# Blocks 2 and 3 of the first x tile: from TensorE transposes to a DMA transpose, with the first weight loads moved to ScalarE

## Chip, cores and metric

One Trainium2 chip; the kernel runs on one core. The metric is device time in microseconds (us), the median of several runs. Lower is better.

## The reference

```python
B, S, D, F = 1, 2048, 1024, 3584          # all bfloat16
def reference(x, w_gate, w_up, w_down):
    return (_gelu(x @ w_gate) * (x @ w_up)) @ w_down   # gelu, tanh form
```

## The kernel before

The 2048 tokens are worked in two halves of 1024, each in two blocks of 512 (`TB`). x is needed with its D axis on the partitions: `xT[tb]` holds eight blocks of 128 rows of D (block 0 is rows 0 to 127) by 512 tokens. For the gate and up products, F is cut into 28 tiles of 128 columns, loaded in chunks of four tiles (`load_w`; a chunk has a gate and an up part). The result stays on chip as `hT`, and the down projection follows for each half.

Most products run by a scheme of seven block products in place of eight (`quads`, `down_group`): sums of blocks of x (`t_sum`, on DVE and ACT) and of the weights (`s_sum`, on GpSimd) are made first. At the start these sums do not exist yet. `first_units` (from line 369) fills that time with plain products: for eight tiles of F and the first 512 tokens it runs over the eight blocks of D. These are the matmuls of line 355, 128x512 each, 16 for each set of two tiles and each of gate and up. I number them p1, p2, ... in the order of PE. The first four blocks' partial sum is also evacuated, since the later scheme uses it: `hold` (line 367), two ScalarE copies for each set and each of gate and up. The same bank then goes on to take blocks 4 to 7 (`rest`), which also ends in the gelu (line 313, ScalarE) and the multiplication (line 318, DVE).

What stands ahead of p1:

- Lines 228 to 236 issue the first loads, on SyncE and ScalarE alike: half of the tokens of x for blocks 0 and 1, weights for blocks 0 and 1 (256 columns; gate on SyncE, up on ScalarE), half of the tokens of x for blocks 2 and 3, the other 256 columns of the weights, and the weights for blocks 2 and 3. x lands untransposed in `xs0`.
- Line 254: seven matmuls on constants (`warm`, line 245) keep TensorE at work until x is there.
- `transpose_x0(0)` (line 337): eight 128x128 TensorE transposes into PSUM, copied to `xT` by DVE (line 345). `transpose_x0(1)` does the same for blocks 2 and 3 behind the first eight products, with one of its copies on ScalarE (line 347).
- Line 258: a DMA transpose (`load_xT`, line 214) brings blocks 4 to 7 on SyncE, and behind it in that queue come the chunk's remaining weights, chunk 1, the second token block of x (two more DMA transposes), and chunk 2.

The order on each engine is the order of the code: every instruction goes through a helper (`pe`, `act`, `dve`, `sp`, `pool`) that chains it behind the one before on its engine. A DMA also waits until the eighth one before it, in the order of the code, has landed, since eight semaphores are used in turn. Eight PSUM banks serve in pairs: `PB` 0 and 1, `VB` 2 and 3, `QB` 4 and 5, `RB` 6 and 7. Set 0 (tiles 0 and 1) uses VB and RB, set 1 (tiles 2 and 3) QB and PB; set 2 is again on QB and PB, set 3 on VB and RB.

In `first_units`, `top(n, j, k0, k1)` is set n, gate (j = 0) or up (j = 1), blocks k0 to k1 - 1, with `hold` where k1 is 4. KPQ is 2, KH is 4, KD is 8:

```python
transpose_x0(0); warm(RB[1], TB // 2)
top(0, 0, 0, KPQ); top(0, 1, 0, KPQ)          # p1-p8
transpose_x0(1)
top(1, 0, 0, KPQ)                             # p9-p12
top(0, 0, KPQ, KH); top(0, 1, KPQ, KH)        # p13-p20, two holds
top(1, 1, 0, KPQ)                             # p21-p24
top(1, 0, KPQ, KH); top(1, 1, KPQ, KH)        # p25-p32, two holds
outs(*rest(1)); outs(*rest(0))                # p33-p64
```

Of the kernel before, what the change touches and what calls it, by code (L numbers as in the profile page):

```python
# [34 lines left out]
def kernel(  # L35
# [8 lines left out]
    nc = tc.nc  # L44
# [6 lines left out]
    KH = KD // 2  # L51
# [5 lines left out]
    FG = 512  # L57
# [3 lines left out]
    TSB = TB // P  # L61
    XQ = 256
    NXQ = D // XQ
    KPQ = XQ // P
# [53 lines left out]
    PB, VB, QB, RB = (0, 1), (2, 3), (4, 5), (6, 7)  # L118
    last_on = {}

    def on(engine, inst):

        if engine in last_on:
            tc.add_manual_dep(
                inst.ins, last_on[engine].ins.name, SCHED_DEP, reason="engine order"
            )
        last_on[engine] = inst
        return inst

    def sp(inst):  # L130
        return on("sp", inst)

    def act(inst):
        return on("act", inst)

    def dve(inst):
        return on("dve", inst)
# [12 lines left out]
    def pe(inst):  # L150
        return on("pe", inst)
# [46 lines left out]
    def load_w(key, j, k0, k1, queue=sp, f0=0, f1=FG):  # L198

        c0 = key[1] * FG  # L200
        eng = nc.scalar if queue is act else nc.sync
        src = (wgv, wuv)[j][:, k0:k1, c0 + f0 : c0 + f1]
        queue(eng.dma_start(out=chunks[key][j][:, k0:k1, f0:f1], in_=src))

    def load_x0(q, queue, ts0=0, ts1=TSB):
        eng = nc.scalar if queue is act else nc.sync
        cols = slice(q * XQ, (q + 1) * XQ)
        src = x2[ts0 * P : ts1 * P, cols].rearrange("(ts p) d -> p ts d", p=P)
        queue(eng.dma_start(out=xs0[:, ts0:ts1, cols], in_=src))

    def load_xT(xT, h, tb, k0, k1):
        t0 = h * SH + tb * TB
        sp(
            nc.sync.dma_start_transpose(
                out=xT[tb][:, k0:k1, :],
                in_=xv[t0 : t0 + TB, k0:k1, :],
            )
        )
# [4 lines left out]
    xT = [None] * NTB  # L223
# [3 lines left out]

    FA = 2 * P
    first = (0, 0)
    for j, queue in enumerate((sp, act)):  # L230
        ts = slice(j * TSB // 2, (j + 1) * TSB // 2)
        load_x0(0, queue, ts.start, ts.stop)
        load_w(first, j, 0, KPQ, queue, 0, FA)
        load_x0(1, queue, ts.start, ts.stop)
        load_w(first, j, 0, KPQ, queue, FA, FG)
        load_w(first, j, KPQ, KH, queue)
    ident = const_pool.tile([P, P], BF16, name="ident")
    make_identity(nc, ident[:])

# [3 lines left out]
    def warm(bank, n=TB):  # L243
        pe(
            nc.tensor.matmul(  # L245
                banks[bank][:, 0:n],
                lhsT=warm_l,
                rhs=warm_r[:, 0:n],
                start=True,
                stop=True,  # L250
            )
        )
# [26 lines left out]
    def t_sum(name, c0=0, c1=KH, on_pool=False):  # L279
        def b(j, l):  # L280
            return xT[l][:, j * KH + c0 : j * KH + c1, :]

        t0 = ("t1", "t2", "t3", "b22", "t4").index(name) * KH * TB
        t = t_mem[:, t0 : t0 + KH * TB].rearrange("p (a b) -> p a b", b=TB)
        tsum[name] = t
        t = t[:, c0:c1, :]
        if name == "b22":
            for c in range(c1 - c0):
                act(nc.scalar.copy(out=t[:, c, :], in_=b(1, 1)[:, c, :]))
            return  # L290
        in0, in1 = {
            "t1": lambda: (b(0, 1), b(0, 0)),
            "t2": lambda: (b(1, 1), tsum["t1"].bitcast(F32)[:, c0:c1, :]),
            "t3": lambda: (b(1, 1), b(0, 1)),
            "t4": lambda: (b(1, 0), tsum["t2"].bitcast(F32)[:, c0:c1, :]),
        }[name]()
        if on_pool:
            pool(nc.gpsimd.tensor_tensor(out=t, in0=in0, in1=in1, op=ALU.subtract))
            return
        dve(nc.vector.tensor_tensor(out=t, in0=in0, in1=in1, op=ALU.subtract))  # L300
# [4 lines left out]
    def gelu(ps, last=False):  # L305

        if last:
            g_sb = new_o(F32)
        else:
            e0 = 4 * CH + (g_ctr[0] % 4) * 2 * TB  # L310
            g_ctr[0] += 1
            g_sb = w_mem[:, e0 : e0 + 2 * TB].bitcast(F32)
        act(nc.scalar.activation(out=g_sb, in_=ps[:], func=ACT.Gelu_apprx_tanh))  # L313
        return g_sb

    def mult(hT, g_sb, ps, fc, tb):
        dve(
            nc.vector.tensor_tensor(  # L318
                out=hT[:, fc, tb * TB : (tb + 1) * TB],
                in0=g_sb,  # L320
                in1=ps[:],
                op=ALU.mult,
            )
        )

    def transpose_x0(q):

        parts = [(KPQ * q, 0, 4), (KPQ * q + 1, 0, 4)]
        over = (QB[1], PB[1])
        if q == 0:  # L330
            parts = [(0, 0, 2), (0, 2, 4), (1, 0, 4)]
            over = (PB[0], PB[1], QB[0])
        for n, (kd, ts0, ts1) in enumerate(parts):
            tp = banks[over[n]][:].bitcast(BF16)
            for ts in range(ts0, ts1):
                pe(
                    nc.tensor.transpose(  # L337
                        tp[:, ts * P : (ts + 1) * P],
                        xs0[:, ts, kd * P : (kd + 1) * P],
                        ident[:],  # L340
                    )
                )
            cols = slice(ts0 * P, ts1 * P)
            if q == 0 or n == 0:
                dve(nc.vector.tensor_copy(out=xT[0][:, kd, cols], in_=tp[:, cols]))
            else:
                act(nc.scalar.copy(out=xT[0][:, kd, cols], in_=tp[:, cols]))

    def plain_products(held, tiles, j, k0, k1):
        for kd in range(k0, k1):  # L350
            for u, t in enumerate(tiles):
                w_sb = chunks[(0, t // FPG)][j]
                f0 = t % FPG * P
                pe(
                    nc.tensor.matmul(  # L355
                        banks[held[u][j]][:],
                        lhsT=w_sb[:, kd, f0 : f0 + P],
                        rhs=xT[0][:, kd, :],
                        start=kd == 0,
                        stop=kd in (KH - 1, KD - 1),  # L360
                        skip_group_check=True,
                    )
                )

    def hold(held, tiles, j):
        for u, t in enumerate(tiles):
            act(nc.scalar.copy(out=p_hold(t, j), in_=bank2(held[u][j])))

    def first_units(hT):

        gs = {}

        def gelus(held, tiles):
            for u, t in enumerate(tiles):
                gs[t] = gelu(banks[held[u][0]])

        def outs(held, tiles):
            for u, t in enumerate(tiles):
                mult(hT, gs[t], banks[held[u][1]], t, 0)

        sets = ((VB, RB), (QB, PB), (QB, PB), (VB, RB))

        def top(n, j, k0, k1):
            tiles = (2 * n, 2 * n + 1)
            plain_products(sets[n], tiles, j, k0, k1)
            if k1 == KH:
                hold(sets[n], tiles, j)

        def rest(n):
            tiles = (2 * n, 2 * n + 1)  # L390
            plain_products(sets[n], tiles, 0, KH, KD)
            gelus(sets[n], tiles)
            plain_products(sets[n], tiles, 1, KH, KD)
            return sets[n], tiles

        transpose_x0(0)
        warm(RB[1], TB // 2)
        top(0, 0, 0, KPQ)
        top(0, 1, 0, KPQ)
        transpose_x0(1)  # L400
        top(1, 0, 0, KPQ)
        top(0, 0, KPQ, KH)
        top(0, 1, KPQ, KH)
        top(1, 1, 0, KPQ)
        top(1, 0, KPQ, KH)
        top(1, 1, KPQ, KH)
        outs(*rest(1))
        outs(*rest(0))
        for j in range(2):
            top(2, j, 0, KH)  # L410
        for j in range(2):
            top(3, j, 0, KH)
        t_sum("t1", 0, KH // 2)
        t_sum("t1", KH // 2, KH)
        t_sum("t2")
        outs(*rest(2))
        t_sum("t3", 0, KH // 2)
        t_sum("b22")
        outs(*rest(3))
        t_sum("t3", KH // 2, KH)  # L420
        t_sum("t4", 0, KH // 2)
        t_sum("t4", KH // 2, KH)
        for j in range(2):
            s_sum(0, MID[0], j, "s3")
        for j in range(2):
            for name in ("s1", "s2"):
                s_sum(0, MID[0], j, name)
        for j in range(2):
            s_sum(0, MID[0], j, "s4")
# [772 lines left out]
```

## Time and profile before

| what | value |
|---|---|
| median of 3 runs | 537.33 us (537.15 to 537.83) |
| profiled execution: time | 538.38 us |
| profiled execution: span, first to last instruction | 536.6 us |
| PE (TensorE matmul) busy | 531.6 us, 99% of the span |
| DVE, ACT, POOL busy | 375.8, 274.2, 257.9 us |
| DMA traffic over the span | 102.69 MB, 191 GB/s |
| p1 starts, p33 starts, p65 starts | 4.78, 13.14, 20.07 us |

Times in a view count from the span's start. PE is TensorE's matmuls, PEld its weight loads, DVE the vector engine, ACT the scalar engine, POOL GpSimd, SP SyncE, and a q behind an engine's name its DMA issues or its other queue work. The chain that ended last is followed back from the last instruction to whatever released each step. A DMA's time to landing counts from the start of its issue.

### The profile page before, as it was taken

How to read it: one execution, taken by the hardware profiler on the slowest of the kernel's cores; microseconds unless marked ns; L12 is line 12 of the kernel's file. 1: busy time of each engine (PE TensorE's matmuls, PEld its weight loads, DVE VectorE, ACT ScalarE, POOL GpSimd, SP SyncE). 2: the span in 40 equal slices, each digit the busy share in tenths (PEclk: the TensorE clock that was granted, in tenths of full speed). 3: DMA queues.
4: the chain of work that ended last, by engine and by line, in shares of the span. 5: the costliest groups of instructions: out<-in, count | busy, mean ns of one | idle time of the engine just before them, and what ended most of it. 6: DMA issues, size and time to landing. Idle time of an engine off the chain costs nothing.

```text
span 536.6 us, 6968 instructions
## 1 busy us (share of the span) xinstructions
PE 531.6 (99%) x2360; PEld 382.4 (71%) x2380; DVE 375.8 (70%) x457; ACT 274.2 (51%) x471; POOL 257.9 (48%) x202
## 2 busy tenths in 40 slices
PE   9999999999999999999999999999999999999997
PEld 4448888887767686776768677776768686766866
DVE  1389988989799997988655343344445469969961
ACT  3466666666464229118455554655555551452280
POOL 0078999998499300000056494958668670000000
PEclk9999999999999999999999999999999999999999
DMA  8973845489892987789941322405041339677946
GB/s 214 267 263 114 240 141 153 120 234 284 227 369 94 346 289 271 241 277 293 327 161 35 123 83 76 133 25 156 1 156 37 121 97 334 215 249 243 290 144 213
DMA packets 97746, 102.69 MB, mean 191 GB/s; under 512 B 18224, under 2 KB 72624, under 8 KB 97712
## 3 DMA queue, kind: packets, MB, share of 16 engines
q1 hardware_dynamic: 73328, 83.57, 49.1%
q10 hardware_dynamic: 24384, 18.68, 11.6%
q8 instruction: 19, 0.31, 0.2%
q14 instruction: 15, 0.12, 0.1%
HBM read 85.98 MB, written 12.58 MB: 184 GB/s over the span
## 4 chain that ended last, share of the span: by engine, by line
PE 98%; DMA 1%; issue 0%; ACT 0%
PE bank L511 60%; PE bank L793 31%; PE bank L355 5%; DMA t_mem<-t_dram 1%; PE bank L245 1%; PE bank L337 0%; ACT o_sb L849 0%
## 5 line engine op out<-in xcount | busy, mean ns | idle before, releaser
L511 PE MATMUL bank<-t_mem,s_mem 128*128 128x512 f32 x1096 | 252.0, 391 | 0.0
L511 PEld LDWEIGHTS bank<-t_mem,s_mem 128*128 128x128 f32 x1096 | 205.7, 188 | 43.6
L462 POOL TENSOR_TENSOR s_mem<-w_mem 128x512 fp32r<-128x512 bf16 x80 | 100.6, 1276 | 177.0 <-DVE t_mem L300 94.7
L318 DVE TENSOR_TENSOR hT<-w_mem,bank 128x512 bf16<-128x512 f32 x106 | 71.0, 683 | 69.7 <-PE bank L511 39.9
L527 DVE TENSOR_TENSOR bank<-bank,m 128x512 f32<-128x512 f32 x112 | 72.3, 693 | 43.3 <-ACT m L567 40.6
L793 PE MATMUL bank<-t_mem,s_mem 128*128 128x512 f32 x416 | 98.4, 394 | 0.2 <-DMA t_mem<-t_dram 0.2
L313 ACT ACTIVATE w_mem<-bank 128x512 f32<-128x512 f32 x106 | 62.6, 597 | 56.8 <-DVE bank L527 36.0
L793 PEld LDWEIGHTS bank<-t_mem,s_mem 128*128 128x128 f32 x416 | 78.0, 188 | 17.7 <-issue 0.6
L511 PE MATMUL bank<-xT,w_mem 128*128 128x512 bf16 x311 | 70.3, 379 | 0.5
L691 DVE TENSOR_TENSOR t_mem<-w_mem 128x1024 fp32r<-128x1024 bf16 x56 | 66.6, 1236 | 0.9 <-PE bank L511 0.9
L462 POOL TENSOR_TENSOR s_mem<-w_mem,s_mem 128x512 fp32r<-128x512 bf16 x46 | 65.5, 1445 | 3.2 <-PE bank L511 3.2
L511 PEld LDWEIGHTS <-w_mem 128*128 128x128 bf16 x320 | 30.6, 98 | 38.0 <-issue 2.4
L462 POOL TENSOR_TENSOR s_mem<-s_mem,w_mem 128x512 fp32r<-128x512 f32 x46 | 55.6, 1229 | 0.2
L572 ACT COPY bank<-bank 128x512 f32<-128x512 f32 x56 | 32.0, 571 | 26.5 <-PE bank L511 21.2
L475 ACT CAST s_mem<-w_mem 128x512 fp32r<-128x512 bf16 x48 | 29.5, 617 | 24.7 <-PE bank L511 23.5
L567 ACT COPY m<-bank 128x512 f32<-128x512 f32 x56 | 32.8, 588 | 15.9 <-PE bank L511 15.9
L793 PEld LDWEIGHTS <-hT 128*128 128x128 bf16 x224 | 21.2, 98 | 26.7 <-issue 2.1
L858 ACT CAST o_sb<-bank 128x512 bf16<-128x512 f32 x27 | 14.8, 586 | 33.8 <-PE bank L793 33.8
L793 PE MATMUL bank<-t_mem,s_late 128*128 128x512 f32 (+1 forms) x132 | 30.3, 382 | 0.0
L537 ACT COPY bank<-bank 128x512 f32<-128x512 f32 x40 | 22.8, 571 | 12.0 <-PE bank L511 12.0
L765 DVE TENSOR_TENSOR s_mem<-hT 128x512 fp32r<-128x512 bf16 (+2 forms) x28 | 23.0, 840 | 8.1 <-PE bank L793 8.1
L793 PEld LDWEIGHTS bank<-t_mem,s_late 128*128 128x128 f32 x132 | 24.4, 188 | 4.9
(61 smaller groups left out, 399.4 us busy)
## 6 DMA issues: line engine op xcount, KB each, us to landing
t_mem<-t_dram SPq DMA_DIRECT2D x56, 512.0 KB, 5.5
wd_sb<-in_w_down_dram SPq DMA_DIRECT2D x26, 512.0 KB, 7.2
t_dram<-o_sb SPq DMA_DIRECT2D x14, 512.0 KB, 3.4
w_mem<-in_w_gate_dram ACTq DMA_DIRECT2D x6, 1024.0 KB, 5.5
w_mem<-in_w_up_dram ACTq DMA_DIRECT2D x6, 1024.0 KB, 7.9
w_mem<-in_w_gate_dram SPq DMA_DIRECT2D x9, 512.0 KB, 5.8
w_mem<-in_w_up_dram SPq DMA_DIRECT2D x9, 512.0 KB, 7.7
w_mem<-in_w_down_dram SPq DMA_DIRECT2D x4, 1024.0 KB, 6.8
```

The lines of the kernel that those rows point to most:

```text
L313: act(nc.scalar.activation(out=g_sb, in_=ps[:], func=ACT.Gelu_apprx_tanh))
L318: nc.vector.tensor_tensor(out=hT[:, fc, tb * TB : (tb + 1) * TB], in0=g_sb, in1=ps[:], op=ALU.mult,)
L355: nc.tensor.matmul(banks[held[u][j]][:], lhsT=w_sb[:, kd, f0 : f0 + P], rhs=xT[0][:, kd, :], start=kd == 0, stop=kd in (KH - 1, KD - 1), s ...
L462: pool(nc.gpsimd.tensor_tensor(out=t, in0=in0, in1=in1, op=op))
L475: act(nc.scalar.copy(out=t, in_=a(1, 1)))
L511: nc.tensor.matmul(banks[bank][:], lhsT=lhs[:, c, :], rhs=rhs[:, c, :], start=start and c == 0, stop=c == KH - 1, skip_group_check=True,)
L527: nc.vector.tensor_tensor(out=banks[dst][:], in0=banks[src][:], in1=m5[:], op=ALU.add)
L567: act(nc.scalar.copy(out=m5[j][:], in_=banks[V_[j]][:]))
L572: act(nc.scalar.copy(out=banks[R_[j]][:], in_=banks[Q_[j]][:]))
L691: dve(nc.vector.tensor_tensor(out=t, in0=in0, in1=in1, op=ALU.subtract))
L765: dve(nc.vector.tensor_tensor(out=t, in0=in0, in1=in1, op=op))
L793: nc.tensor.matmul(banks[bank][:, c0:c1], lhsT=lhs(i, u), rhs=rhs(i)[:, c0:c1], start=start and i == 0, stop=stop and i == NS - 1, skip_gr ...
```

## The change

SyncE now issues, in this order: half of the tokens of x for blocks 0 and 1; a DMA transpose of blocks 2 and 3, all 512 tokens (256 KB), straight into `xT`; the gate weights and the up weights for blocks 2 and 3; and then, as before, the DMA transpose of blocks 4 to 7 and all that follows. ScalarE issues the other half of x and then the four quarter parts of the weights for blocks 0 and 1. x for blocks 2 and 3 is no longer loaded untransposed, and the second set of eight TensorE transposes and their two copies are gone. The sixteen products on blocks 0 and 1 (both sets, gate and up) now come first, the sixteen on blocks 2 and 3 behind them, so that the four holds follow each other. All from `rest(1)` on has its order.

```diff
-    for j, queue in enumerate((sp, act)):
-        ts = slice(j * TSB // 2, (j + 1) * TSB // 2)
-        load_x0(0, queue, ts.start, ts.stop)
-        load_w(first, j, 0, KPQ, queue, 0, FA)
-        load_x0(1, queue, ts.start, ts.stop)
-        load_w(first, j, 0, KPQ, queue, FA, FG)
-        load_w(first, j, KPQ, KH, queue)
+    load_x0(0, sp, 0, TSB // 2)
+    load_xT(xT, 0, 0, KPQ, KH)
+    load_x0(0, act, TSB // 2, TSB)
+    for f0 in (0, FA):
+        for j in range(2):
+            load_w(first, j, 0, KPQ, act, f0, f0 + FA)
+    for j in range(2):
+        load_w(first, j, KPQ, KH)
...
-    def transpose_x0(q):
-
-        parts = [(KPQ * q, 0, 4), (KPQ * q + 1, 0, 4)]
-        over = (QB[1], PB[1])
-        if q == 0:
-            parts = [(0, 0, 2), (0, 2, 4), (1, 0, 4)]
-            over = (PB[0], PB[1], QB[0])
-        for n, (kd, ts0, ts1) in enumerate(parts):
+    def transpose_x0():
+
+        over = (PB[0], PB[1], QB[0])
+        for n, (kd, ts0, ts1) in enumerate(((0, 0, 2), (0, 2, 4), (1, 0, 4))):
...
-            if q == 0 or n == 0:
-                dve(nc.vector.tensor_copy(out=xT[0][:, kd, cols], in_=tp[:, cols]))
-            else:
-                act(nc.scalar.copy(out=xT[0][:, kd, cols], in_=tp[:, cols]))
+            dve(nc.vector.tensor_copy(out=xT[0][:, kd, cols], in_=tp[:, cols]))
...
-        transpose_x0(0)
+        transpose_x0()
         warm(RB[1], TB // 2)
-        top(0, 0, 0, KPQ)
-        top(0, 1, 0, KPQ)
-        transpose_x0(1)
-        top(1, 0, 0, KPQ)
-        top(0, 0, KPQ, KH)
-        top(0, 1, KPQ, KH)
-        top(1, 1, 0, KPQ)
-        top(1, 0, KPQ, KH)
-        top(1, 1, KPQ, KH)
+        for k0 in (0, KPQ):
+            for n in range(2):
+                for j in range(2):
+                    top(n, j, k0, k0 + KPQ)
```

## The prediction

> **What bounds the kernel now.** I read the page first. PE is busy for 531.6 of 536.6 us, and the chain that ended last is PE for 98%; so only PE's own instructions and the moments at which PE waits count.
>
> ```profile
> PE 531.6 (99%) x2360; PEld 382.4 (71%) x2380; DVE 375.8 (70%) x457; ACT 274.2 (51%) x471; POOL 257.9 (48%) x202
> ...
> PE 98%; DMA 1%; issue 0%; ACT 0%
> ```
>
> The change touches the first 20 us alone. So next came the timeline of PE, and that of the weight loads (PEld), which show waits that matmuls hide:
>
> ```profile
> 0.77 3.15 PE L245 MATMUL bank<-const-bfloat16-1.0 128*128 128x512 bf16 x7 [0.77 <-PEq L1186]
> 3.71 1.06 PE L337 MATMUL bank<-ident,w_mem 128*128 128x128 bf16 x8
> 4.57 0.42 PE L245 MATMUL bank<-const-bfloat16-1.0 128*128 128x256 bf16 x1
> 4.78 2.79 PE L355 MATMUL bank<-xT,hT 128*128 128x512 bf16 x8
> 7.41 0.61 PE L337 MATMUL bank<-ident,w_mem 128*128 128x128 bf16 x8
> ...
> 6.49 0.58 PEld L355 LDWEIGHTS <-hT 128*128 128x128 bf16 x3 [0.28 <-issue]
> 7.19 0.65 PEld L337 LDWEIGHTS <-w_mem 128*128 128x128 bf16 x8
> 7.80 0.59 PEld L355 LDWEIGHTS <-hT 128*128 128x128 bf16 x4
> 8.81 0.76 PEld L355 LDWEIGHTS <-hT 128*128 128x128 bf16 x5 [0.43 <-DMA hT<-in_w_gate_dram]
> ```
>
> Columns: start, length, engine, line, instruction; in brackets the idle time before and what ended it. PE is never idle after 0.77. Products p1 to p5 start at 4.78, 5.21, 5.63, 6.06 and 6.49, that is 0.43 us apart; from p6 on the step is 0.216 (64 products from 20.07 to 33.89). PE thus runs at half speed until about 6.6 us. One wait is visible: p13's weights land late (8.81), which makes its step 0.31 instead of 0.216. Third, the queues:
>
> ```profile
> 0.74 0.45 SPq L209 DMA_DIRECT2D w_mem<-in_x_dram  x1
> 1.24 0.46 SPq L203 DMA_DIRECT2D hT<-in_w_gate_dram  x1
> ...
> 4.69 4.21 SPq L214 DMA_TRANSPOSE xT<-in_x_dram  x1
> 8.96 0.57 SPq L203 DMA_DIRECT2D hT<-in_w_gate_dram  x1
> ```
>
> The four-block transpose holds SyncE for 4.21 us, 1.05 a block, and the gate weights for rows 512 to 1023 leave only behind it.
>
> **The change, part by part.** Times are those of the profiled execution: span 536.6, 538.38 in all.
>
> *Removed from PE:* the second set of eight transposes. It takes PE from 7.41 to 7.85: **-0.44**. With it go one copy on DVE (0.42) and one on ACT (0.59); neither is on the chain.
>
> *p13's wait* (0.31 - 0.216 = 0.10) goes: those weights, issued at 3.62 and landed 5.1 us later, are now first read by p17, at 7.19 + 9 x 0.216 = 9.13: **-0.10**.
>
> *The order* puts four evacuations of ACT (L367, two copies each) behind p20, p24, p28 and p32, which are 4 x 0.216 = 0.86 us apart. A pair of copies takes more:
>
> ```profile
> 9.67 1.07 ACT L367 COPY hT<-bank 128x512 f32<-128x512 f32 x2 [1.03 <-PE bank L355]
> 10.63 0.61 ACT L367 COPY s_late<-bank 128x512 f32<-128x512 f32 x1
> ```
>
> Two copies start 9.67, the third 10.63: 0.48 each, 0.96 a pair. Before, four other products lay between the second and third pair, and ACT caught up. After: the first copy starts 0.04 after p19's end (9.56 + 0.38), at 9.98; the sixth at 9.98 + 5 x 0.48 = 12.38, and ends 0.61 later, 12.99. p34 overwrites that bank, and would be ready at 7.19 + 26 x 0.216 = 12.81; it starts near 13.04. Before, the sixth copy (the second of the pair 12.26 + 1.07) ended at 13.33 and p34 started at 13.39, 0.03 behind its turn. **+0.2**. All PE work behind queues on it.
>
> *Weights from ScalarE.* p1 needs its gate weights by 4.57 (its weight load). Before, they were SyncE's second issue (1.24, landed after 3.2, at 4.42); now they are ACT's second, whose row is 1.25 and 3.4, so 4.67, and p1 comes 0.1 late. Bounds: nothing, and what an ACT issue loses beside transposes. ACT's 512 KB gate loads show that: issued at 72.00, 90.08 and 108.22,
>
> ```profile
> hT<-in_w_gate_dram ACTq DMA_DIRECT2D x1, 512.0 KB, 4.1
> ...
> hT<-in_w_gate_dram ACTq DMA_DIRECT2D x1, 512.0 KB, 5.9
> ...
> w_mem<-in_w_gate_dram ACTq DMA_DIRECT2D x1, 512.0 KB, 5.4
> ```
>
> The first has no transpose near; the others were issued while SyncE issued two (at 89.19 and 90.38; at 107.82 and 109.81): 1.3 to 1.8 more. But there a 512 KB load of w_down was also ahead. A lone block, issued at 134.79, sends its first packets at 136.0, 1.2 us on; so the gate issue, at the same moment as the transpose, should be ahead of most of it. I take **+0.2**, between 0 and +1.8. The next weights are needed later each time: up by 6.4, second gate part 7.4, up 8.2. ACT's third and fourth issues landed at 1.79 + 4.8 = 6.6 and 2.31 + 5.1 = 7.4 behind x, which now isn't ahead of them; the fifth was never so early. I take no wait; at worst 0.2.
>
> *The transpose, blocks 2 and 3.* Issue 1.24 + 2 x 1.05 = 3.35; the four-block one landed 2.1 us after its issue ended (4.69 + 6.3 = 11.0 against 8.90), so about 5.5; p17 needs it at 9.13. Rows of any transpose run from 2.7 us (one block, 134.79) to 9.3 (14.86, behind 2 MB of weights): 3.9 to 10.5. I take no wait; at most +1.4. It is one queue, so no transpose waits for another.
>
> *SyncE behind it.* It loses two x and two weight issues and gains 2.1 us: two 256 KB weight issues end near 4.4 (the second needs ACT's x, landed 3.9), the four-block transpose starts near 4.45 instead of 4.69 and ends at 8.66. The gate weights behind it landed at 12.54; now 12.3, and p33 needs them at 7.19 + 25 x 0.216 = 12.59. If the short transpose takes 0.6 longer to issue, p33 waits 0.3; between nothing and +0.5. Chunk 1 was issued at 11.22, landed 6.8 later, and is read at 20.07: 2 us to spare.
>
> Sum: -0.44 - 0.10 + 0.2 + 0.2 = **-0.15 us**. Later PE work moves with it: the one later wait of PE is 0.2 us for a DMA whose issue follows PE. The profiled execution (538.38) is 1.05 above the median (537.33). Forecast: 538.2 for such an execution, **537.2** as a median, 536.7 to 537.9 by this case alone. About 0.2% (1.07 us) is what a measurement of this kernel can tell from no change.
>
> **Rivals.**
>
> *Full gain.* Nothing is late and the copies overlap more: -0.54, 536.8. For it: x's second load, whose two halves took 4.7 and 4.8 us against 2.9 and 3.2 for the first, leaves the queues. Against: the copies' 0.96. It stays within 0.2%.
>
> *The first weights queue behind the transpose (slower).* Place: p1. Price: the 1.3 to 1.8 above put the landing at 6.0 to 6.5, p1 late by 1.4 to 1.9; with the -0.34 of the other terms that is +1.1 to +1.6, 538.4 to 538.9. It makes the kernel measurably slower from a lateness of 1.4 us. PE is then also idle while still at half speed. If full speed waits for unbroken work (0.77 to 6.6, 5.8 us, here), starting over costs up to 5.8/2 = 2.9 more. For it: both rows. Against: the w_down load ahead of both.
>
> The Trainium skill (DMA: Bandwidth & Descriptors, Issuing engines are not separate DMA queues) says that issues of ScalarE and SyncE run on the same 16 DMA engines and interleave, and that two issuers save only issue time; this speaks against what the move to ScalarE could give, and the two rows agree. The Trainium skill (TensorE: Matmul & The Clock Gate, Part 1) says that full speed comes after a busy window of about 3.4 us that runs freely; by it, one missed window would cost an estimated 3.4/2 = 1.7 us, and where the window falls changes from run to run.
>
> *The transpose lands late.* Place: p17. At the 9.3 row, +1.4 - 0.34: 538.4. Against: 3.6 us of slack over the 5.5.
>
> **How the numbers follow.** Forecast 0.62; full gain 0.10; weights behind the transpose 0.20; late transpose 0.04; other, either side, 0.04. Slower by over 0.2%: nine tenths of the second rival, half of the third, some of the rest: 0.22. Faster by over 0.2% needs 1.07 of a possible 0.54, so only an earlier full speed gives it: 0.06. Within: 0.72. Range 536.4 (full gain and some scatter) to 538.9 (the second rival without the speed's loss).
>
> **What would show it.** PE's timeline: eight transposes, then p1 at 4.8 to 5.0 (5.9 or later: second rival); the 0.43 us steps end near 6.6; sixteen products without a break; no idle ahead of p17 (else third rival); a step of about 0.4 at p34; DMA rows: ACT's second issue landing after some 3.4 us, SyncE's short transpose holding it for 2.1. Wrong if the first 20 us gain or lose over 0.5 us elsewhere, or if anything past 34 us changes.

## The result and the profile after

The changed kernel takes 538.62 us (median of 11 runs, 538.02 to 539.93) against 537.48 for the kernel before (11 runs, 537.15 to 538.60): ratio 1.0020, 95% interval 1.0011 to 1.0028. It is slower, by 1.1 us. A repeat (e13 below) gave 538.48 against 537.61, ratio 1.0021 (1.0012 to 1.0030).

The page of the changed kernel's profile (span 536.9, time 538.65) shows PE less busy (531.6 before), and 1% of the chain that ended last is now on ACT:

```profile
PE 530.5 (99%) x2352; PEld 382.0 (71%) x2372; DVE 376.7 (70%) x456; ACT 273.4 (51%) x470; POOL 258.9 (48%) x202
...
PE 97%; DMA 1%; ACT 1%; issue 0%; ACTq 0%
```

In its lines L334, L349, L361 and L500 are what L337, L355, L367 and L511 were. The timeline of PE (start, length, instruction, idle time before):

```profile
3.71 1.06 PE L334 MATMUL bank<-ident,w_mem 128*128 128x128 bf16 x8
4.57 0.42 PE L246 MATMUL bank<-const-bfloat16-1.0 128*128 128x256 bf16 x1
4.78 1.17 PE L349 MATMUL bank<-xT,hT 128*128 128x512 bf16 x4
7.10 13.45 PE L349 MATMUL bank<-xT,hT 128*128 128x512 bf16 x59 [1.15 <-DMA hT<-in_w_up_dram]
```

and that of the weight loads:

```profile
5.14 0.31 PEld L349 LDWEIGHTS <-hT 128*128 128x128 bf16 x2 [0.21 <-issue]
7.09 1.41 PEld L349 LDWEIGHTS <-hT 128*128 128x128 bf16 x8 [1.64 <-DMA hT<-in_w_up_dram]
```

p1 is not late. p1 to p4 take 1.17 us, since full speed (0.216 us a product) starts with p2 (5.14) in this execution. p5 would follow at 5.78; it starts at 7.10, because the first up weights land at 7.05. The chain in order of time (start, length, what; idle pieces are "issue") says which issue that is, and shows the copies:

```profile
1.79 5.26 DMA hT<-in_w_up_dram
7.05 0.05 issue
7.10 3.50 PE bank L349 x15
10.59 0.02 issue
10.62 1.07 ACT hT L361 x2
11.69 0.03 ACT s_late L361
11.72 0.34 issue
12.05 1.60 ACT hT L361 x3
13.66 0.04 issue
13.70 0.38 PE bank L349
```

It is ScalarE's third issue (1.79). Behind p19 ACT's copies carry the chain as far as p34, which starts at 13.70, 0.26 behind its turn (p33 at 13.22, and 0.216 for it). SyncE's queue:

```profile
0.74 0.45 SPq L209 DMA_DIRECT2D w_mem<-in_x_dram  x1
1.25 1.33 SPq L214 DMA_TRANSPOSE xT<-in_x_dram  x1
...
4.00 5.11 SPq L214 DMA_TRANSPOSE xT<-in_x_dram  x1
9.15 0.58 SPq L203 DMA_DIRECT2D hT<-in_w_gate_dram  x1
```

The two profiles differ by only 0.3 us (538.65 - 538.38; p65 at 20.39 and 20.07), the medians by 1.1. The experiments had to explain the rest too. In nearly all profiles below, time less p65's start is 518.2 within 0.4 (519.3 in e13), so p65's start is a fair reading of a profiled execution. It is a reading of that execution alone, not of the median.

### The profile page after: what moved, and what is told of

It is laid out like the page before. It is cut to its first block, busy times and chain, and to the rows that moved or that the text cites. A ratio compares the mean times of both kernels' runs of the same rounds, so it can differ in the third digit from the quotient of the medians.

```text
span 536.9 us, 6944 instructions
## 1 busy us (share of the span) xinstructions
PE 530.5 (99%) x2352; PEld 382.0 (71%) x2372; DVE 376.7 (70%) x456; ACT 273.4 (51%) x470; POOL 258.9 (48%) x202
## 4 chain that ended last, share of the span: by engine, by line
PE 97%; DMA 1%; ACT 1%; issue 0%; ACTq 0%
PE bank L500 60%; PE bank L782 33%; PE bank L349 4%; DMA hT<-in_w_up_dram 1%; ACT hT L361 0%; ACTq L203 0%; ACTq L209 0%; ACT o_sb L838 0%; ACT s_late L361 0%
## 5 line engine op out<-in xcount | busy, mean ns | idle before, releaser
L500 PE MATMUL bank<-t_mem,s_mem 128*128 128x512 f32 x1096 | 252.0, 391 | 0.0
L500 PEld LDWEIGHTS bank<-t_mem,s_mem 128*128 128x128 f32 x1096 | 205.8, 188 | 43.5
L451 POOL TENSOR_TENSOR s_mem<-w_mem 128x512 fp32r<-128x512 bf16 x80 | 101.7, 1293 | 176.2 <-DVE t_mem L301 94.6
L500 PE MATMUL bank<-xT,w_mem 128*128 128x512 bf16 x310 | 70.3, 379 | 0.5
L500 PEld LDWEIGHTS <-w_mem 128*128 128x128 bf16 x320 | 30.6, 98 | 38.0 <-issue 2.4
```

The costliest lines, as they stand in the source:

```text
L451: pool(nc.gpsimd.tensor_tensor(out=t, in0=in0, in1=in1, op=op))
L500: nc.tensor.matmul(banks[bank][:], lhsT=lhs[:, c, :], rhs=rhs[:, c, :], start=start and c == 0, stop=c == KH - 1, skip_group_check=True,)
```

## The experiments

Each timed run is a median of 11 or 12 executions beside before's on the same chip; intervals are about 0.09% (0.5 us) either side, so only what profiles and times say together is used.

**What moves from run to run.** e1 and e9 are the kernel before, unchanged; e10 and e13 the changed kernel.

> The kernel before, once more, for a second profile. In its first profile the half-speed steps of TensorE (0.43 us) lasted until 6.6 us; in that of the changed kernel full speed began at 5.1 us, so that the two profiles differ by 0.3 us where the medians differ by 1.1. If the start of full speed moves from run to run (theory: chance of the run), a second profile shows it elsewhere between some 4 and 7.5 us, and the span moves by up to 0.8 us with it; the time stays within 0.3 us of before. If the change itself brought full speed forward (rival), it is at 6.6 us again.

537.81 against 537.66, ratio 1.0001 (0.9992 to 1.0010). Its profile (538.19) has full speed from 6.5 again: the rival's reading for now.

> A third profile of the kernel before. Theory: two things vary from run to run in the first 9 us, when full speed starts (6.6 and 6.5 us in the first two profiles) and when the gate weights of blocks 2 and 3 land (8.8 and 7.6 us), and p13 starts at the later of the two; a run near the median (537.5) has p13 near 8.0, against 8.8 and 8.4 in the two profiles, which were of slow runs (538.4, 538.2). Then time less p65's start is 518.2 within 0.4 in this one too. Rival: the first 20 us are the same in all runs and the spread comes from later.

537.91. Timeline of PE:

```profile
4.72 1.93 PE L355 MATMUL bank<-xT,hT 128*128 128x512 bf16 x8
7.09 0.68 PE L337 MATMUL bank<-ident,w_mem 128*128 128x128 bf16 x8 [0.43 <-DMA w_mem<-in_x_dram]
7.83 6.46 PE L355 MATMUL bank<-xT,hT 128*128 128x512 bf16 x28
```

Here full speed starts by 5.2, but the early start is lost again: the second transposes wait for x's second load (landed 7.22). p13 came near 8.7, not 8.0 as expected. p65 is at 19.96. So the start of full speed does move (6.6, 6.5, 5.2, and 4.7 in e4), and the kernel before has a wait for a third issue of its own.

> A second profile of the changed kernel. Theory: ScalarE's up weights land at 6.8 to 7.3 us again and p5 starts there, whether full speed starts early or not; p65 at 20.2 to 20.5. Rival: the late landing was a chance of one run, and p5 starts before 6.6.

538.00. Here ScalarE's third issue took 4.3 us, and p5 started at 6.15, 0.4 late: p65 at 19.68. The rival holds; the landing varies by chip or by execution.

> The changed kernel once more, on the chip of the three runs beside it. Theory (p5 starts at the landing of ScalarE's third issue, and this moves from run to run: 7.05 and 6.10 us in its two profiles): slower than before by 0.4 to 1.3 us, and p5's wait in the profile agrees with the time within 0.4. Rival (the loss is a chance of the first call): within 0.2 of before.

538.48, ratio 1.0021 (1.0012 to 1.0030). The up weights landed at 6.86, p5 started at 6.91, 1.1 late, and p34 again 0.26 late. The profiled execution (539.46) also lost 0.3 us at 55.7 and 0.5 at 269.1, which the two other profiles of the changed kernel do not show.

**What makes p5 wait.** The edits are against the changed kernel, except in e5. The first puts the up weights that p5 reads on SyncE, ahead of the transpose.

```diff
     load_x0(0, sp, 0, TSB // 2)
+    load_w(first, 1, 0, KPQ, sp, 0, FA)
     load_xT(xT, 0, 0, KPQ, KH)
...
-    for f0 in (0, FA):
-        for j in range(2):
-            load_w(first, j, 0, KPQ, act, f0, f0 + FA)
+    load_w(first, 0, 0, KPQ, act, 0, FA)
+    for j in range(2):
+        load_w(first, j, 0, KPQ, act, FA, FG)
```

> The changed kernel, but the up weights of the first 256 columns (128 KB) are SyncE's second issue, ahead of the short transpose, and no longer ScalarE's third. Theory (the wait of p5 for these weights is the whole loss, 1.3 us): they land near 4.7 us, p5 follows p4 without a break, and the time is 1.0 to 1.4 us under the changed kernel's, that is from 0.4 under to 0.1 above before. Rival (anything late only moves the wait on): p9 waits for the next gate weights, now ScalarE's third issue, which land at 7.0 or later, and less than 0.6 us is won back.

537.94 against 537.66, ratio 0.9998 (0.9989 to 1.0007): the loss is gone. But the waits moved on, as the rival said, though to p13 and p33 and not to p9; the timeline of PE:

```profile
4.78 3.28 PE L350 MATMUL bank<-xT,hT 128*128 128x512 bf16 x12
8.38 4.49 PE L350 MATMUL bank<-xT,hT 128*128 128x512 bf16 x20 [0.32 <-DMA hT<-in_w_up_dram]
13.12 1.25 PE L350 MATMUL bank<-xT,hT 128*128 128x512 bf16 x4 [0.25 <-DMA hT<-in_w_gate_dram]
```

p5 follows p4; p13 waits 0.48 and p33 0.41. With the copies repaired too (below, e14's edit):

> Both repairs: the up weights that p5 reads as SyncE's second issue ahead of the transpose, and the second copies on DVE. Theory: no wait of p5 and none of p34; what remains are p13's and p33's waits for weights behind the transposes (0.5 and 0.4 us in the profile of the first repair alone); time 0.2 to 0.6 us under before. Rival (each wait only moves on): within 0.15 of before or above it.

538.62 against 537.61, ratio 1.0016 (1.0007 to 1.0025). My theory fell: p13 waited 1.06 us for ScalarE's fourth issue (landed 8.41, 6.1 us after it) and p33 0.17. Those weights landed no earlier in e2 (8.34), so the profiles do not explain why e2's median is 0.7 lower; the two ran on different chips. Putting one weight load ahead of the transpose is no reliable repair.

Next, the transpose behind the plain weight loads:

```diff
     load_x0(0, sp, 0, TSB // 2)
-    load_xT(xT, 0, 0, KPQ, KH)
...
     for j in range(2):
         load_w(first, j, KPQ, KH)
+    load_xT(xT, 0, 0, KPQ, KH)
```

> The changed kernel, but the short transpose is issued behind the two 256 KB weight loads for blocks 2 and 3 on SyncE, so that ScalarE's issues run beside plain loads alone. Theory A (the transpose's packets hold the DMA engines, and ScalarE's third issue lands 5.3 us after its issue for that reason): the up weights land at 6.0 us or before, p5 waits 0.3 us at most, p17 waits for the transpose (landing 7.5 to 9), and the time is 0.7 to 1.3 us under the changed kernel's. Theory B (a third issue on a queue takes some 5 us whatever is beside it, as x's second load took 4.8 before): they land at 6.6 us or later again and p5 waits 0.9 us or more.

538.26 against 537.66, ratio 1.0013 (1.0004 to 1.0021). Theory B holds: with 512 KB of weights in the transpose's place the up weights still landed at 6.69, and p5 started at 6.74, 1.03 late.

A plain load of the same x in its place (the comment stands for the edit of the products, which is left out):

```diff
-    load_xT(xT, 0, 0, KPQ, KH)
+    load_x0(1, sp, 0, TSB)      # x plain, 256 KB; second PE transposes behind p8, p9 to p16 as in the change
```

> The changed kernel's queues and order of products, but in the short transpose's place SyncE issues a plain 256 KB load of the same x, and TensorE transposes it behind p8 as before. Theory (third issue): ScalarE's up weights land at 6.5 to 7.1 again and p5 waits 0.8 to 1.4 us with full speed early. Rival (the transpose's packets): they land by 6.0. Either way what is left against the changed kernel's 5.3 us to landing is the transpose's part. Time: within 0.4 us of the changed kernel's by the theory, 1 us or more under it by the rival.

538.27 against 537.47, ratio 1.0017 (1.0008 to 1.0026). The up weights landed at 6.54; p1 waited too (5.39; its gate weights landed at 5.34), which hid p5's wait. e7, on the same chip, has the transpose in that place and landed them at 7.10: 0.56 later. DMA in the stretch 3.2 to 5.6 us, first of the changed kernel, then of e6 (q10 is ScalarE's queue: packets, MB, share of the engines):

```profile
DMA packets 1319, 0.41 MB, mean 169 GB/s; under 512 B 1018, under 2 KB 1319, under 8 KB 1319
...
q10 hardware_dynamic: 320, 0.15, 36.6%
```

```profile
DMA packets 1254, 0.74 MB, mean 308 GB/s; under 512 B 65, under 2 KB 1254, under 8 KB 1254
...
q10 hardware_dynamic: 679, 0.33, 49.4%
```

About the same number of packets, but the transpose's are of 256 bytes. All queues together moved 0.33 MB less in 2.4 us, and ScalarE's queue less than half as much. The 0.56 is not the price of a transpose at equal bytes, though: the plain load takes SyncE less time to issue, so that e6 has another 256 KB of weights (issued at 1.75, in e7 at 2.63) ahead of the up weights (1.79).

The kernel before with a swap on ScalarE's queue alone, x's second half load and the first up weights:

```diff
-        load_w(first, j, 0, KPQ, queue, 0, FA)
+        if j == 0:
+            load_w(first, j, 0, KPQ, queue, 0, FA)
         load_x0(1, queue, ts.start, ts.stop)
+        if j == 1:
+            load_w(first, j, 0, KPQ, queue, 0, FA)
```

> The kernel before with one swap on ScalarE's queue: x's second load is its second issue, and the up weights that p5 reads its third (as in the changed kernel). No transpose, no other change. Theory (a queue's third issue at the start lands 4 to 5 us after it, at 5.8 to 6.7, whatever is beside it): p5 waits for them, by 0.1 to 1.0 us depending on when full speed starts, its step is above 0.5 us in the profile, and the time is 0.2 to 0.8 us above before. Rival (only the transpose makes the third issue late): they land by 5.5, p5's step stays at 0.43 or 0.22 and the time is that of before.

537.69 against 537.47, ratio 1.0002 (0.9994 to 1.0011). The up weights landed at 6.20 and p5 waited 0.45, as the theory said; the time did not follow, because p13 waits for the gate weights of blocks 2 and 3 (8.82) in this order anyway.

The last one holds SyncE's transpose, and all behind it on SyncE, until the fifth warm matmul has ended:

```diff
     load_x0(0, sp, 0, TSB // 2)
-    load_xT(xT, 0, 0, KPQ, KH)
...
-    for j in range(2):
-        load_w(first, j, KPQ, KH)
...
     for i in range(NWARM):
         warm(i)
+        if i == 4:
+            held_back = last_on["pe"]
+    load_xT(xT, 0, 0, KPQ, KH)
+    tc.add_manual_dep(last_on["sp"].ins, held_back.ins.name, SYNC_DEP, reason="held back")
+    for j in range(2):
+        load_w(first, j, KPQ, KH)
```

> The changed kernel, but SyncE's short transpose, and all behind it on SyncE, wait for the fifth of the seven warm matmuls (end at 3.1 us), so that ScalarE's issues have only x ahead of and beside them until then. Theory (what counts is how many bytes are ahead: 768 KB when the up weights land 6.5 to 7.1, 512 KB here): ScalarE's third issue lands by 5.7 and p5 waits 0.1 us at most; in exchange the four-block transpose is issued 1.2 us later and p33 waits for the weights behind it, 0.5 to 1.3 us, so that the time is within 0.5 of the changed kernel's. Rival (the rank in the queue counts): it lands at 6.2 or later and p5 waits 0.5 us or more.

537.81 against 537.98, ratio 1.0000 (0.9991 to 1.0008): no loss. This run tells the rank in the queue and the bytes apart. ScalarE's third issue from issue to landing, in the changed kernel, in e3, in e6 and here:

```profile
hT<-in_w_up_dram ACTq DMA_DIRECT2D x1, 128.0 KB, 5.3
```

```profile
hT<-in_w_up_dram ACTq DMA_DIRECT2D x1, 128.0 KB, 4.9
```

```profile
hT<-in_w_up_dram ACTq DMA_DIRECT2D x1, 128.0 KB, 4.8
```

```profile
hT<-in_w_up_dram ACTq DMA_DIRECT2D x1, 128.0 KB, 3.4
```

Same rank in the queue, 256 KB less ahead than in the changed kernel: it landed at 5.22. In the stretch of above, ScalarE's queue moved three times as much as in the changed kernel:

```profile
q10 hardware_dynamic: 1023, 0.49, 73.3%
```

The chip is not the reason. e18 ran on the same one, and there ScalarE's third issue, with 896 KB asked for up to then, took 5.4 us. But bytes ahead are not told apart from bytes beside, since all of SyncE's later loads were held back too. PE's timeline then has no wait to speak of before p33:

```profile
4.73 7.17 PE L354 MATMUL bank<-xT,hT 128*128 128x512 bf16 x32
12.10 2.12 PE L354 MATMUL bank<-xT,hT 128*128 128x512 bf16 x9 [0.20 <-DMA hT<-in_w_gate_dram]
```

p33 waited 0.36, less than the 0.5 to 1.3 expected, and the time came out at before's, not within 0.5 of the changed kernel's.

Taken together: the versions in which p5 waited a microsecond or more were slower than before (the changed kernel, e13, e3, e7, and by less e14), and so was e15, with such a wait at p13. Those without (e2, e12, e17) were not. e6 is slower in another way, with p1 0.4 late and half speed until 6.2.

**What the order and its copies cost.** The order alone, in the kernel before (second transposes still behind p8):

> The kernel before with its loads and its TensorE transposes, but with the sixteen products on blocks 0 and 1 first (the second transposes stay behind p8), so that the four pairs of copies follow each other. Theory: the copies of ScalarE hold p34 for 0.2 to 0.3 us and nothing else changes; time 0.1 to 0.3 us above before, or less where p13's wait for weights (0.1) goes. Rival: the order is free, step of p34 under 0.26 us and time equal to before.

537.27 against 537.66, ratio 0.9991 (0.9983 to 1.0000). The copies were not seen to cost anything here: p33 started 0.26 late, but for its gate weights (landed 12.29), and the time fell instead of rising. A likely reason is that the order gives the weights of blocks 2 and 3 more time.

> Before with the new order of the products alone, again on another chip. Theory: the order takes p13's wait for the gate weights of blocks 2 and 3 away and adds 0.26 at p34; sum 0 to 0.5 us under before, as in the first run (0.4). Rival: that run was chance, and the order alone costs 0.1 to 0.3.

537.42 against 537.61, ratio 0.9996 (0.9987 to 1.0005): p34 started 0.26 late, as said; no loss again, and no gain that is settled.

> The changed kernel with the old order of the products (p13 to p16 are set 0 on blocks 2 and 3, as before). Theory: p5 waits as in the changed kernel, then p13 waits for the gate weights of blocks 2 and 3 (landing 8.6 to 8.9) by 0.1 us or less and p34 by 0.05 instead of 0.26; time 0 to 0.3 us under the changed kernel's. Rival (the new order is what saves, as order alone took 0.4 us off before): 0.2 us or more above it.

538.25 against 537.47, ratio 1.0016 (1.0006 to 1.0027). The wait of p34 fell to 0.03, p13 did not wait, p5 started at 7.15. So the new loads, with the old order, make the kernel slower by themselves.

The second copy of each of the first four evacuations on DVE:

```diff
         for u, t in enumerate(tiles):
-            act(nc.scalar.copy(out=p_hold(t, j), in_=bank2(held[u][j])))
+            if t < 4 and u == 1:
+                dve(nc.vector.tensor_copy(out=p_hold(t, j), in_=bank2(held[u][j])))
+            else:
+                act(nc.scalar.copy(out=p_hold(t, j), in_=bank2(held[u][j])))
```

> The changed kernel with the second copy of each of the four first evacuations on DVE. Theory: p34's wait of 0.26 us goes and nothing else: 0.2 to 0.3 us under the changed kernel, 0.8 to 1.0 above before. Rival: the gate weights behind the four-block transpose (landed 12.8) hold p33 then, and nothing is won.

537.66 against 537.82, ratio 0.9996 (0.9987 to 1.0004), not slower at all. It ran on the chip of e10, where the up weights landed at 5.86 and p5 did not wait; so it says nothing of the copies against the changed kernel's 538.62. Beside the changed kernel on one chip:

> The changed kernel with the second copy of each evacuation on DVE, beside the changed kernel itself. Theory: 0.2 to 0.3 us under it (p34's wait in its profiles is 0.26). Rival (the copies' wait is hidden behind other waits): equal to it within 0.15. If it is 0.5 or more under it, my account of the loss is wrong.

537.94, ratio 1.0009 (1.0000 to 1.0018), 0.54 under the changed kernel on the same chip. That is just past the 0.5 that I had named as speaking against my account. The two intervals (each 0.09% either way) do not tell 0.54 from 0.26, and from p5 to p65 the profiles differ by 0.14 (13.22 and 13.08, the latter with a wait of p9 of 0.12): 0.26 for the copies. I keep 0.26 and call the rest open.

> Before with the new order of the products and with the second copy of each of the four first evacuations on DVE. Theory: p34 (or p33) no longer waits for the copies, 0.26 us in the order-only run, and the slack that the order gives to the weights of blocks 2 and 3 stays: 0.5 to 0.8 us under before. Rival: the wait moves to weights (p33 reads the gate weights behind the four-block transpose): 0.2 to 0.4 under before, as with the order alone.

537.81 against 537.82, ratio 0.9996 (0.9988 to 1.0005). p17 and p33 waited for weights (0.33 and 0.18) instead: the rival's way, without its gain.

**A version with both undone.** SyncE: x, up, gate for blocks 2 and 3, the transpose, up for blocks 2 and 3; ScalarE: x, gate, gate, up; second copies on DVE.

> A candidate: the up weights that p5 reads are SyncE's second issue, then the gate weights of blocks 2 and 3, the short transpose and the up weights; ScalarE issues x, gate, gate, up. The second copy of each of the four first evacuations is on DVE, which has nothing to do then. Theory: no wait of p5, no wait of p34, eight transposes less; p9 and p13 wait for third and fourth issues by 0.3 us at most; time 0.3 to 0.9 us under before. Rival (what is taken from one product's weights is taken from the next): p9, p13, p17 or p33 waits 0.5 us or more and the time is within 0.2 us of before.

537.22 against 537.47, ratio 0.9994 (0.9985 to 1.0003): 0.25 under, less than the 0.3 to 0.9 expected. p65 at 19.16, with 0.2 us of waiting, at p1.

> The candidate once more, on another chip: 0.25 us under before in its first run, its interval reaching from 0.8 under to 0.15 above. Theory: again 0 to 0.6 us under before, with no wait of PE between p1 and p65 above 0.3 us. Rival: the first run was chance and it is at or above before.

537.50 against 537.98, ratio 0.9991 (0.9982 to 1.0000). No wait is above 0.3 us, as expected. Twice under before, by 0.25 and 0.5 us, each interval ending at or past 1: better than the change, and perhaps than before.

## Why the prediction was wrong

The forecast was 0.15 us faster; measured is 1.1 slower. The range held it, but the sign was wrong. The price of the second rival (538.4 to 538.9), which had 0.20, held it too; that is luck, since this rival had the wrong place (below).

- **The step that failed** is "The next weights are needed later each time ... I take no wait; at worst 0.2". p5 waited 1.3, 1.1 and 0.4 us for them in the three profiles of the changed kernel. I let ScalarE's third issue off because x was no longer ahead of it. But the transposed x is the same 256 KB, issued earlier. Before, x's own third issue landed 4.8 us after its issue with 768 KB asked for up to then, itself included. The changed kernel asks for 768 KB too; that row was the price, and it gives 6.6. e3 and e6 (1024 KB, all plain: 4.9 and 4.8) and e17 (512 KB: 3.4) show that the bytes on both queues count. They are a rough price only: 768 KB with the loads of before took 4.0 (e4) to 5.4 us (e9), and in e2 and e15, with 896 KB but the transpose issued no earlier than 1.75, the third issue took 4.2 and 4.4. What the transpose adds is not settled: the weights landed at 7.10 in e7, against 6.54 in e6, but at 6.10 in e10 and 5.86 in e12.
- **A second error in the same step**: the time at which p5 is ready, 6.49, was read from one execution that ran at half speed until 6.6. At full speed from 5.1 it is 5.78. With 6.49 the wait would have been 0.6; it was 1.3. More than half of the wait is this.
- **The second rival** had the mechanism but the wrong place: p1's weights came at 4.64 (4.67 worked out) and cost nothing; p5's are the late ones. Its extra price did not come: after 1.15 us of idle PE went on in 0.216 us steps.
- *Copies*: 0.2 expected at p34, 0.26 measured. *Eight transposes*: p9 follows p8 with no gap, 0.44 as said. *p13*: its old wait went as said (the same weights landed at 8.60, and p17, which now reads them first, started at 9.77); but p13 now reads ScalarE's fifth issue (landed 8.85) and waited 0.06 for that.
- *The short transpose*: 1.33 us to issue, not 2.1; landed at 7.28, not 5.5, inside the bounds, and hidden before p17 (9.8). *SyncE behind it*: the four-block transpose held it for 5.11 us, not 4.21; the gate weights landed at 12.79 (12.3 expected), hidden only because PE was late by then; where PE was less late (e2, e17), p33 waited.
- *Small slips*: the four terms add up to -0.14, and the lone block's first packets come at 136.1. Neither bears on the result.

Why the profiles show 0.3 and the medians 1.1 can be worked out, but is not shown. The same third landing L costs before less. In e9, L is x, read behind p8, with 56 products and eight transposes to go: p65 is L + 12.7 (7.22, 19.96). In the changed kernel L is p5's weights, with 60 products and the copies' wait to go: L + 13.3 (7.05, 20.39; 6.86, 20.13), and 13.6 in e10 (6.10, 19.68), where p9 waited too. That is 0.6; with the 0.56 between e7 and e6, a single pair, it would make 1.1. The first profile of before, and the two others, are of executions above its median (538.38, 538.19, 537.91), with late full speed or a late x. e4 and e16 have before's loads with x at 5.8 and 6.5 and the gate weights of blocks 2 and 3 at 7.9; from there p13 at 7.9 and 52 products give p65 near 19.2, a time of 537.4. No profile of so fast a run of before was taken.

The Trainium skill (DMA: Bandwidth & Descriptors, Issuing engines are not separate DMA queues) was borne out: moving weights to ScalarE gave them no engines of their own, and ScalarE's queue moved 0.15 MB beside SyncE's transpose where it moved 0.49 with SyncE held back. The Trainium skill (Advanced Engine Details and Errata, X-Bar Transpose (TRN2)) says that transpose DMAs are as fast as regular ones; here the stretch with the transpose moved 169 GB/s against 308 with a plain load, and the transpose took 6.0 us to land against 3.5 for the plain load, so the measurement decides against it (277 GB/s in e10 and e12, so not to this extent in every run).

## What to carry to other kernels

When a load is replaced by another that brings the same bytes earlier, what is issued at the same time can stand behind those bytes, on whichever queue. Price each later load by a row with as many bytes asked for up to then, on both queues, as a first estimate, and ask which product reads the last of them first. Read the readiness of the consumer from more than one execution where the start of full speed moves. A wait removed early in a PE-bound kernel pays only up to the next landing.

## What the hardware showed

- Full speed of PE started between 4.7 and 6.6 us in the profiles, for the same warm matmuls from 0.77; it moves from run to run, as the Trainium skill (TensorE: Matmul & The Clock Gate, Part 1) has it, and an idle of 1.15 us did not end it. It is read from the steps (0.43 and then 0.216 us a product): the granted clock in the profile's rows is 1.00 throughout the first 20 us, before and after.
- With the transpose in front, ScalarE's third issue took 4.1 and 4.3 us in two profiles on one chip and 5.1 to 5.3 in the four others. The chip need not be the reason: on that same chip, with the loads of before, x's third issue took 5.4 (e9) and 4.3 (e11). One profile, or one chip, can show a loss of 1 us that others do not.
- A 256 KB transpose as the queue's second issue took 4.8 to 6.0 us to land (six profiles), a plain load of the same x in its place 3.5 (e6), and the transpose held back to 3.10 took 4.0 (e17).
